# Seven block products in place of eight for the back products of the last layer's slice pairs

## The chip, the cores and the metric

The kernel runs on one core of a Trainium2 chip. The time is device microseconds (us) of one execution. A profile is one more execution, recorded by the hardware profiler; its span runs from the first to the last recorded instruction. PE is the matmul engine (TensorE), DVE is VectorE, ACT is ScalarE, POOL is GpSimd, SP issues DMAs.

## The reference, cut to what matters

```python
y = irfft(rfft(x, axis=1) * F)              # x is (2, 3008, 256), so 6016 tokens of 256
h = sigmoid(y @ w_gate) * (y @ w_val)       # 256 -> 1536
x2 = h @ w_out                              # 1536 -> 256
u = x2 @ w_in2                              # 256 -> 2048   (the last layer)
g = u * sigmoid(1.702 * u)
out = g @ w_out2                            # 2048 -> 256   (its back products)
```

Only the last layer, and in it the product `g @ w_out2`, is changed.

## The kernel before, in words

All matmuls are fp32-exact by splitting: each operand is a high part (rounded to the fp32r type) and a low part (what is left), and `mm3` makes three matmuls of a product: high by high, high by low, low by high. A tile has tokens along its columns: `tiles2` is ten tiles of 512 tokens and two of 448. Channels lie on the 128 partitions.

The last layer is the loop over `p` (six tile pairs, two tiles of tokens each) and, inside, over `fp` (eight slice pairs: 256 of the 2048 inner channels, two slices of 128). One pass, called a **set** here, makes a 2 by 2 product of blocks (two tiles, two halves of the 256 inputs, two slices). It is made with seven block products in place of eight, a scheme of Strassen's kind: sums of the inputs ("forms") were made ahead by DVE, sums of the weights too. The products go through `prod(o, k, first)`, in this order: `x` 0, `y` 4, `x` 5, `z` 1, `x` 6, `y` 2, `x` 3, where `x`, `y`, `z`, `w` are PSUM banks, and between them DVE and ACT do the sums that the scheme wants:

- after `x` 0: ACT copies the bank `x` to `s1`; product 5 is then accumulated onto the same bank;
- after `y` 4: ACT copies `y` to `s5`;
- after `x` 5: DVE makes `y = x + s5` (line 1772); after `z` 1: `z = z + s1` (line 1774); after `x` 6: `w = x + s5` (line 1782).

The four results `z`, `w`, `y`, `x` are the blocks (slice 0, tile 0), (1, 1), (0, 1), (1, 0). `Block.act` applies the activation twice by ACT: into the high part (line 1692) and in full precision into a tile `sg` (line 1693, two buffers); `Block.low` subtracts them by POOL (line 1696, both operands in SBUF). Then `Block.back(c)` multiplies a block by the output weights of its slice, half `c`, and accumulates in one of four PSUM banks `accs[tile][c]` (banks 4 to 7): eight back products a set, which are queued (`held`, `queue`) and issued by `back()` between the products of the next set. So a set has 15 groups of three matmuls on PE.

The order on every engine is that of the code: nothing is moved by a scheduler. "Chores" are pieces of other work that `spend(chores, n)` places at three points of a set, so many as `rate` says: in the last layer's later pairs, the forms of the next tile pair (DVE subtractions of SBUF tiles, ACT copies).

Of the kernel before, what the change touches and what calls it, by code (L numbers as in the profile page):

```python
# [17 lines left out]
P = 128  # L18
# [9 lines left out]
FC1 = DFF1 // P  # L28
# [61 lines left out]
def kernel(  # L90
# [1446 lines left out]
    def next_decode(j):  # L1537
        return decode_chores(j, st, lambda: [w[:, j % NWL] for w in wl] + [sp])

    def spend(q, n):  # L1540
        for k in range(n):
            if not q and bulk and not hold_back:
                q.extend(next_decode(bulk.pop(0)))
            if k and q and getattr(q[0], "apart", False):
                return
            chore(q)
# [5 lines left out]
    for p in range(FIRST, nt // 2):  # L1552
        n = tiles[2 * p][3]
        rhs = [[h[:, :n] for h in d] for d in sets[p]]
        for f in range(FC1):
# [8 lines left out]
            def prod(o, k, first):  # L1564
                mm3(o, lhs[k], rhs[k], first, True, skip_group_check=True)
# [114 lines left out]
    assert gn[0] % 4 == 0  # L1680
    gn[0] = 0

    class Block:
        def __init__(self, i, j, p, fp, bank):
            self.i, self.j, self.t, self.fp, self.bank = i, j, 2 * p + j, fp, bank
            self.n = tiles2[self.t]
            self.own = p == 0 and i == 0 and (fp > 0 or j == 0)

        def act(self):
            self.gp = [x[:, :self.n] for x in gslot()]  # L1690
            self.sg = self.bank if self.own else work.tile([P, 512], F32, tag="sg", name="sg")[:, :self.n]
# [3 lines left out]
        def low(self):  # L1695
            (nc.vector if self.own else nc.gpsimd).tensor_sub(self.gp[1], self.sg, self.gp[0].bitcast(F32))  # L1696

        def back(self, c):
            t, n, f = self.t, self.n, 2 * self.fp + self.i
            end = self.fp == FC2 // 2 - 1 and self.i != self.j  # L1700
            acc = accs[self.j][c][:, :n]
            mm3(acc, wp(f, c), self.gp, self.fp == 0 and self.i == self.j, end)
# [16 lines left out]
    LAST_S = 4  # L1719
    for p in range(nt // 2):  # L1720
        n = tiles2[2 * p]
        rhs = [[h[:, :n] for h in d] for d in (setB if p % 2 == 0 else setA)]
        asked = p + 1 == nt // 2
        for fp in range(FC2 // 2):
            x, z, w = (ps[ROT[(nset + k) % 3]][:, :n] for k in range(3))
            y = ps[2][:, :n]
            bz, by, bw, bx = (Block(i, j, p, fp, o) for (i, j), o in zip(((0, 0), (0, 1), (1, 1), (1, 0)), (z, y, w, x)))
            nset += 1
            if fp == 0:
                hold_back = False  # L1730
                while p and chores:
                    chore(chores)
            if p == 0:
                for g in (0, 1, 4, 5, 6, 2, 3):
                    if (fp or g not in (2, 3)) and 2 * g in done and g not in summed:
                        reload_s(g)
                for q in range(FC1):
                    if q in done and q not in placed:
                        reload(q)
                assert {2 * fp, 2 * fp + 1} <= placed and fp in summed  # L1740
                while 2 * fp + 1 not in done:
                    spend(chores, 1)
            lhs = w_parts(fp)
# [22 lines left out]
            queue += held  # L1766
            prod(y, 4, True)
            nc.scalar.copy(s5[:, :n], y)
            spend(chores, rate[0])
            back()  # L1770
            prod(x, 5, False)
# [5 lines left out]
            back()  # L1777
            spend(chores, rate[1])
# [7 lines left out]
            bw.low()  # L1786
            prod(y, 2, False)
# [10 lines left out]
            blocks = (bz, bw, by, bx) if fp or p == 0 else (bw, bz, by, bx)  # L1798
            held = [lambda o=o, c=c: o.back(c) for o in blocks for c in range(2)]
    queue += held  # L1800
    while queue:
        back()
# [41 lines left out]
```

## Time and profile before

| | before |
|---|---|
| time, median of 3 runs | 1134.05 us (1134.01 to 1134.63) |
| the profiled execution | 1133.56 us |
| its span | 1131.8 us |
| PE busy, matmul instructions | 1124.5 us (99%), 5072 |
| DVE, ACT, POOL busy | 694.0 us (61%), 641.6 us (57%), 408.9 us (36%) |
| mean granted clock of PE | 0.999 |

The profiled execution is 0.49 us under the median; 1.76 us of it lie outside the span. Busy time of an engine is an average over stages: DVE is busier in the first part of the program than in the last layer.

### The profile page before, as it was taken

The numbers are of one execution on the slowest core, as the hardware profiler recorded it, in microseconds if no ns is written. First come the engines' busy times: TensorE is split into PE (matmuls) and PEld (weight loads), VectorE is DVE, ScalarE is ACT, GpSimd is POOL, SyncE is SP. The second block draws the span as 40 slices with busy tenths as digits, with TensorE's granted clock in tenths as the row PEclk, the third lists the DMA queues.
The fourth block names the chain that finished last, engine by engine and source line by source line (L and its number), as shares of the span: only waits on it lengthen the run. The fifth ranks groups of instructions, "written<-read, shape, count | busy, mean of one in ns | idle before, by whom it ended". The sixth has DMA issues, their size and how long they took to land.

```text
span 1131.8 us, 14614 instructions
## 1 busy us (share of the span) xinstructions
PE 1124.5 (99%) x5072; PEld 905.0 (80%) x5072; DVE 694.0 (61%) x1171; ACT 641.6 (57%) x1221; POOL 408.9 (36%) x351
## 2 busy tenths in 40 slices
PE   9999999999999999999999999999999999999998
PEld 4378887677888888888888878888888888888897
DVE  6989998786688756787788788533224233233211
ACT  4655555554455644555655666756556556555554
POOL 3810004654333311211211132344555445544444
PEclk9999999999999999999999999999999999999999
DMA  9755238893200300126056250010100200200100
GB/s 208 200 182 180 93 122 226 195 182 80 80 1 1 109 1 1 41 94 118 31 191 210 95 178 31 28 47 1 57 19 1 75 1 1 70 1 1 38 1 33
DMA packets 84009, 91.21 MB, mean 81 GB/s; under 512 B 39072, under 2 KB 55968, under 8 KB 83936
## 3 DMA queue, kind: packets, MB, share of 16 engines
q1 hardware_dynamic: 81968, 87.37, 27.5%
q10 hardware_dynamic: 1968, 2.91, 0.8%
q8 instruction: 40, 0.66, 0.2%
q14 instruction: 33, 0.27, 0.1%
HBM read 55.52 MB, written 30.80 MB: 76 GB/s over the span
## 4 chain that ended last, share of the span: by engine, by line
PE 92%; DVE 2%; issue 1%; ACT 0%; DMA 0%; POOL 0%; ACTq 0%; DVEq 0%; POOLq 0%
PE ps L124 31%; PE ps L125 30%; PE ps L126 30%; PE ps L324 1%; DMA yraw<-tt 0%; DVE z L500 0%; DVE a L534 0%; DVE yp L1132 0%; POOL g L1696 0%; DVE ap L540 0%; DVE yraw L512 0%; DVE yraw L743 0%; DVE ps L560 0%; POOL v L550 0%; DVE v L479 0%
## 5 line engine op out<-in xcount | busy, mean ns | idle before, releaser
L1696 POOL TENSOR_TENSOR g<-sg,g 128x512 fp32r<-128x512 f32 (+1 forms) x117 | 150.0, 1295 | 178.4 <-ACT sg L1693 162.6
L1772 DVE TENSOR_TENSOR ps<-ps,tabs 128x512 f32<-128x512 f32 (+1 forms) x48 | 33.0, 688 | 213.4 <-PE ps L126 213.4
L121 POOL TENSOR_TENSOR g<-sg,g 128x512 fp32r<-128x512 f32 (+1 forms) x47 | 59.5, 1266 | 257.2 <-ACT g L120 257.2
L124 PE MATMUL ps<-yp,wg 128*128 128x512 f32 (+2 forms) x382 | 149.8, 393 | 0.0
L125 PE MATMUL ps<-yp,wg 128*128 128x512 f32 (+2 forms) x382 | 147.8, 387 | 0.0
L126 PE MATMUL ps<-yp,wg 128*128 128x512 f32 (+2 forms) x382 | 147.8, 387 | 0.0
L1692 ACT ACTIVATE g<-ps 128x512 fp32r<-128x512 f32 (+1 forms) x128 | 76.2, 595 | 84.6 <-DVE ps L1774 58.4
L125 PE MATMUL ps<-g,wo 128*128 128x512 f32 (+1 forms) x288 | 110.9, 386 | 0.0
L124 PE MATMUL ps<-g,wo 128*128 128x512 f32 (+1 forms) x288 | 110.9, 386 | 0.0
L126 PE MATMUL ps<-g,wo 128*128 128x512 f32 (+1 forms) x288 | 110.7, 386 | 0.0
L1696 POOL TENSOR_TENSOR wo<-sg,wo 128x512 fp32r<-128x512 f32 (+1 forms) x60 | 77.1, 1294 | 82.8 <-ACT sg L1693 82.6
L1693 ACT ACTIVATE sg<-ps 128x512 f32<-128x512 f32 (+1 forms) x177 | 105.5, 596 | 1.2 <-POOL g L1696 0.9
L124 PEld LDWEIGHTS ps<-yp,wg 128*128 128x128 f32 x382 | 71.7, 188 | 26.2 <-issue 13.0
L126 PEld LDWEIGHTS ps<-yp,wg 128*128 128x128 f32 x382 | 71.7, 188 | 14.3
L125 PEld LDWEIGHTS ps<-yp,wg 128*128 128x128 f32 x382 | 71.7, 188 | 13.0 <-issue 0.2
L124 PE MATMUL ps<-g,wg 128*128 128x512 f32 (+1 forms) x192 | 73.9, 385 | 0.0
L125 PE MATMUL ps<-g,wg 128*128 128x512 f32 (+1 forms) x192 | 73.9, 385 | 0.0
L126 PE MATMUL ps<-g,wg 128*128 128x512 f32 (+1 forms) x192 | 73.9, 385 | 0.0
L1629 ACT ACTIVATE sg<-ps 128x480 f32<-128x480 f32 (+1 forms) x48 | 28.1, 586 | 70.9 <-DVE ps L1627 70.9
L1692 ACT ACTIVATE wo<-ps 128x512 fp32r<-128x512 f32 (+1 forms) x64 | 38.2, 596 | 44.4 <-DVE ps L1774 30.3
L124 PEld LDWEIGHTS ps<-g,wo 128*128 128x128 f32 x288 | 54.0, 188 | 11.1 <-issue 0.8
L126 PEld LDWEIGHTS ps<-g,wo 128*128 128x128 f32 x288 | 54.0, 188 | 10.5
(304 smaller groups left out, 2778.4 us busy)
## 6 DMA issues: line engine op xcount, KB each, us to landing
yscr<-tt SPq DMA_DIRECT2D x56, 128.0 KB, 2.2
raw<-in_w_out_dram SPq DMA_DIRECT2D x14, 512.0 KB, 4.0
yraw<-xscr SPq DMA_DIRECT2D x14, 512.0 KB, 4.5
x<-in_xd_dram SPq DMA_DIRECT2D x32, 192.0 KB, 4.0
wscr<-wl SPq DMA_DIRECT2D x24, 256.0 KB, 2.0
wg<-wscr SPq DMA_DIRECT2D x24, 256.0 KB, 2.9
out_dram<-yraw SPq DMA_DIRECT2D x20, 256.0 KB, 2.2
f<-in_fd_dram SPq DMA_DIRECT2D x23, 192.0 KB, 4.6
```

Of the source, the lines that this page charges most:

```text
L121: lo_eng.tensor_sub(dst_lo, src, dst_hi.bitcast(F32))
L124: nc.tensor.matmul(out=o, lhsT=w[0], rhs=x[0], start=first, stop=False, **kw)
L125: nc.tensor.matmul(out=o, lhsT=w[0], rhs=x[1], start=False, stop=False, **kw)
L126: nc.tensor.matmul(out=o, lhsT=w[1], rhs=x[0], start=False, stop=last, **kw)
L324: nc.tensor.matmul(out=o[c], lhsT=w[64 * r:64 * r + n], rhs=x(r, k), start=True, stop=True, tile_position=(64 * r, 64 * k),)
L1629: nc.scalar.activation(out=sgz, in_=z, func=AF.Sigmoid)
L1692: nc.scalar.activation(out=self.gp[0], in_=self.bank, func=AF.Gelu_apprx_sigmoid)
L1693: nc.scalar.activation(out=self.sg, in_=self.bank, func=AF.Gelu_apprx_sigmoid)
L1696: (nc.vector if self.own else nc.gpsimd).tensor_sub(self.gp[1], self.sg, self.gp[0].bitcast(F32))
L1772: nc.vector.tensor_add(y, x, s5[:, :n])
```

## The change: what it does

The back product of a set is itself a 2 by 2 product of blocks (two tiles, two slices, two halves of the outputs). In some sets it is now made with seven block products too. These sets are `fp` 1, 2, 4 and 5 in the tile pairs `p` 2 to 5, and `fp` 4 and 5 in `p` 1: 18 sets, always two neighbours. I call the two the **first** and the **second** set, and the set behind them (`fp` 3 or 6) the **third**; `fp` 0 and 7 are plain, as is all of `p` 0.

- **Class Seven.** `after_y` and `after_x` make sums of the activated blocks instead of using them as they are: `t1 = y - z`, `t2 = w - t1`, `t3 = w - y`, `t4 = x - t2`, by DVE; their high parts by ACT copies (line 1733); the low parts of `t1`, `t2`, `t3` by POOL, those of `x` and `t4` by DVE. `third` and `fourth` do the high parts of `t3` and `t4` in the set after.
- **The products** `backs`: m3, m1, m6, m2, m7, m4, m5. Four of them (m1, m6, m7, and m5) go to the PSUM bank 3, `chain`; after each, `keep` reads that bank by DVE and adds it to one of four SBUF sums (`sums`; line 1868, or 1866 the first time). At `fp` 7 `fold` adds the sums to the accumulators by six DVE additions (line 1901).
- **Banks.** Bank 3 is taken by the chain. So for all sets of `p` 1 to 5 `x` and `z` alternate over two banks, and `w` is an `sg` tile in SBUF.
- **Weight sums.** `out_sums` makes the sums of the output weights of four slice pairs as chores in `p` 1 and at the beginning of `p` 2 (lines 1782 to 1799), and writes them to DRAM; `load_sout` loads three of them (six DMAs of 64 KB on SP's queue) for each of the 18 sets.
- **Rates** of the chores in `p` 1 to 5 are changed.

```diff
+    SEVEN = (1, 2, 4, 5)
+    OUT = {(1, 1): 4, (1, 2): 5, (1, 3): 1, (2, 0): 2}
...
+        def after_y(self):
+            z, y = self.z, self.y
+            y.full()
+            nc.vector.tensor_sub(z.sg, y.sg, z.sg)
+            self.t1.sg = z.sg
+            self.t1.high()
+            self.t1.low()
+
+        def after_x(self):
+            z, w, x, y = self.z, self.w, self.x, self.y
+            nc.vector.tensor_sub(self.e[0], w.sg, y.sg)
+            self.t3.sg = self.e[0]
+            nc.vector.tensor_sub(w.sg, w.sg, z.sg)
+            self.t2.sg = w.sg
+            x.take()
+            nc.scalar.activation(out=x.gp[0], in_=x.bank, func=AF.Gelu_apprx_sigmoid)
+            x.full()
+            x.low(nc.vector)
+            self.t2.high()
+            self.t2.low()
+            nc.vector.tensor_sub(self.e[1], x.sg, self.t2.sg)
+            self.t4.sg = self.e[1]
...
+            def keep(k):
+                dst = self.sums[k]
+                if not self.begun:
+                    nc.vector.tensor_copy(dst, self.chain)
+                else:
+                    nc.vector.tensor_add(dst, dst, self.chain)
...
+            return [m3, m1, m6, m2, m7, m4, m5]
...
-            rate = (2, 1, 1) if p else (3, 2, 2) if fp else (0, 0, 0)
+            if p:
+                if (p, fp) in OUT:
+                    out_jobs.append(OUT[p, fp])
+                if seven:
+                    rate = (0, 0, 0) if was else (3, 3, 0)
+                elif was:
+                    rate = 0, 1, 3
+                else:
+                    rate = (2, 2, 0) if fp == 0 else (0, 3, 3) if fp == LAST else (3, 3, 2) if fp == 3 else (2, 2, 2)
...
             nc.scalar.copy(s1[:, :n], x)
+            if was:
+                was.third()
...
             nc.scalar.copy(s5[:, :n], y)
+            if was:
+                was.fourth()
             spend(chores, rate[0])
...
+            if was:
+                was.fourth_low()
...
             spend(chores, rate[1])
             if not bz.own:
                 bz.low()
             prod(x, 6, False)
-            nc.vector.tensor_add(w, x, s5[:, :n])
+            if p:
+                bw.bank = bw.hold()
+            nc.vector.tensor_add(bw.bank, x, s5[:, :n])
...
-            by.act()
-            spend(chores, rate[2])
-            by.low()
+            if seven:
+                if was:
+                    load_sout(fp, 1)
+                seven.after_y()
+            else:
+                by.act()
+                spend(chores, rate[2])
+                by.low()
             prod(x, 3, False)
-            bx.act()
-            bx.low()
-            back()
+            if seven:
+                back()
+                seven.after_x()
+            else:
+                bx.act()
+                bx.low()
+                back()
             back()
```

What stands where on DVE, between the middle of a second set and the beginning of a third (`p` 3, `fp` 5 and 6). Before, one set in the same tile pair (line 1132 is a chore):

```order
L1772 TENSOR_TENSOR ps_73<-ps_71,tabs 128x512 [waits PE_49,Activation_49]
L1774 TENSOR_TENSOR ps_72<-ps_72,s_2834 128x512 [waits PE_49]
L1132 TENSOR_TENSOR sx_2826<-yraw,sx_2825 128x512
L1782 TENSOR_TENSOR ps_74<-ps_71,tabs 128x512 [waits PE_49]
L1132 TENSOR_TENSOR sx_2826<-yraw,sx_2825 128x512 [waits DVE_49,Activation_49]
```

Now (the second set's `w` sum is line 2008, line 1737 with `spare` is t4's low part, line 1134 a chore; `ps_74` is the chain):

```order
L2008 TENSOR_TENSOR sg<-ps_72,tabs 128x512 [waits PE_49,Pool_49]
L1868 TENSOR_TENSOR sums<-sums,ps_74 128x512 [waits PE_49]
L1825 TENSOR_TENSOR sg<-ps_73,sg 128x512 [waits Activation_49,Pool_49]
L1868 TENSOR_TENSOR sums<-sums,ps_74 128x512 [waits PE_49]
L1832 TENSOR_TENSOR spare<-sg,ps_73 128x512
L1834 TENSOR_TENSOR sg<-sg 128x512 [waits DVE_49,Pool_49]
L1737 TENSOR_TENSOR g_2873<-ps_72,g_2872 128x512 [waits Activation_49]
L1842 TENSOR_TENSOR spare<-ps_72,sg 128x512 [waits DVE_49]
L1868 TENSOR_TENSOR sums<-sums,ps_74 128x512 [waits PE_49]
L1992 TENSOR_TENSOR ps_73<-ps_71,tabs 128x512 [waits PE_49,Activation_49]
L1994 TENSOR_TENSOR ps_72<-ps_72,s_2835 128x512 [waits PE_49]
L1868 TENSOR_TENSOR sums<-sums,ps_74 128x512 [waits PE_49]
```

Between two sets' own sums there was one chore or none; now a `keep` (line 1868) that waits for m5, the last group of the set, stands ahead of the subtractions for t3 (1832) and t2 (1834), and the latter has both inputs in SBUF.

ACT at the same place; before, two activations, each twice, and then the copy to `s1`:

```order
L1692 ACTIVATE wo_85<-ps_73 128x512 [waits PE_49]
L1693 ACTIVATE sg<-ps_73 128x512 [waits Pool_49]
L1127 ACTIVATE yp_2639<-xs 128x448
L1692 ACTIVATE wo_85<-ps_71 128x512 [waits PE_49]
L1693 ACTIVATE sg<-ps_71 128x512 [waits Pool_49]
L1760 COPY s_2834<-ps_72 128x512 [waits PE_49]
```

Now (line 1728 `y` and `x` in full, 1733 the high parts of t1, t2, t3, 1837 the high part of `x`):

```order
L1728 ACTIVATE ps_73<-ps_73 128x512 [waits PE_49]
L1733 ACTIVATE wo_86<-sg 128x512 [waits DVE_49]
L1837 ACTIVATE ks_1645<-ps_72 128x512 [waits PE_49,Pool_49]
L1728 ACTIVATE ps_72<-ps_72 128x512
L1733 ACTIVATE g_2872<-sg 128x512 [waits DVE_49]
L1970 COPY s_2835<-ps_71 128x512 [waits PE_49]
L1733 ACTIVATE wo_86<-spare 128x512
```

The copy to `s1` (line 1970) now stands behind the high part of t2, which waits for DVE.

DVE in `p` 1, `fp` 1, where the weight sums are made; these rows are new, and a plain set had no work there before but its three sums:

```order
L1992 TENSOR_TENSOR ps_73<-ps_72,tabs 128x512 [waits PE_49,Activation_49]
L1994 TENSOR_TENSOR ps_71<-ps_71,s_2835 128x512 [waits PE_49]
L1792 TENSOR_TENSOR wr<-wv 128x128
L1793 TENSOR_TENSOR wr<-wv,wr 128x128 [waits DVE_49]
L1799 TENSOR_TENSOR wlo<-wr,wh 128x512 [waits Activation_49]
L2008 TENSOR_TENSOR sg<-ps_72,tabs 128x512 [waits PE_49,Pool_49]
```

The low part of the weight sums (line 1799, both inputs in SBUF) stands ahead of the sum into `w` (2008).

## Rows read from the trace of the kernel before

**Rows 1.** The page: busy time by engine; busy time of stretches of the last layer.

```profile
PE 1124.5 (99%) x5072; PEld 905.0 (80%) x5072; DVE 694.0 (61%) x1171; ACT 641.6 (57%) x1221; POOL 408.9 (36%) x351
745.00:827.00 82.00, 82.00 (x363) 67.91 (x362) 27.17 (x37) 47.38 (x89) 41.82 (x33) 1.00 0.08 26
909.00:991.00 82.00, 82.00 (x364) 67.89 (x363) 27.15 (x37) 47.77 (x90) 41.58 (x32) 1.00 0.08 25
```

**Rows 2.** Waits from 640 to 1132 us, those of PE's weight loads (all).

```profile
PEld ps L124 <- ACT s L1760: 0.5, 1, 0.5
PEld ps L124 <- ACT sg L1693: 0.5, 1, 0.5
PEld ps L124 <- DVE ps L1772: 0.4, 1, 0.4
PEld ps L124 <- DVE g L1696: 0.2, 1, 0.2
```

**Rows 3.** Timeline, PE: start, duration, then what (512 columns; 448 columns).

```profile
848.15 0.39 PE L124 MATMUL ps<-sx,wo 128*128 128x512 f32 x1
848.37 0.39 PE L125 MATMUL ps<-sx,wo 128*128 128x512 f32 x1
848.60 0.39 PE L126 MATMUL ps<-sx,wo 128*128 128x512 f32 x1
848.83 0.39 PE L124 MATMUL ps<-sx,wg 128*128 128x512 f32 x1
...
1090.22 0.36 PE L124 MATMUL ps<-g,wg 128*128 128x448 f32 x1
1090.42 0.36 PE L125 MATMUL ps<-g,wg 128*128 128x448 f32 x1
```

**Rows 4.** Timeline of one set, DVE, ACT and POOL; in brackets idle time and releaser.

```profile
849.10 0.70 DVE L1772 TENSOR_TENSOR ps<-ps,tabs 128x512 f32<-128x512 f32 x1 [5.85 <-PE ps L126]
849.71 0.70 DVE L1774 TENSOR_TENSOR ps<-ps,s 128x512 f32<-128x512 f32 x1
850.31 0.68 DVE L1132 TENSOR_TENSOR yp<-yraw,yp 128x512 fp32r<-128x512 f32 x1
851.75 0.70 DVE L1782 TENSOR_TENSOR ps<-ps,tabs 128x512 f32<-128x512 f32 x1 [0.75 <-PE ps L126]
852.35 1.09 DVE L1132 TENSOR_TENSOR yp<-yraw,yp 128x512 fp32r<-128x512 f32 x1
850.44 0.60 ACT L1692 ACTIVATE wo<-ps 128x512 fp32r<-128x512 f32 x1 [1.14 <-DVE ps L1774]
850.93 0.59 ACT L1693 ACTIVATE sg<-ps 128x512 f32<-128x512 f32 x1
851.61 1.29 POOL L1696 TENSOR_TENSOR wo<-sg,wo 128x512 fp32r<-128x512 f32 x1 [4.37 <-ACT sg L1693]
```

**Rows 5.** Timeline around a wait of PE for the copy to s1.

```profile
653.31 0.58 ACT L1760 COPY s<-ps 128x512 f32<-128x512 f32 x1
653.43 0.40 PE L126 MATMUL ps<-g,wg 128*128 128x512 f32 x1
653.94 0.51 PE L124 MATMUL ps<-sx,wo 128*128 128x512 f32 x1
654.28 0.39 PE L125 MATMUL ps<-sx,wo 128*128 128x512 f32 x1
```

**Rows 6.** Timeline, DVE and POOL where both work at once.

```profile
793.89 1.65 DVE L1132 TENSOR_TENSOR sx<-xs,sx 128x512 fp32r<-128x512 f32 x1 [1.65 <-ACT sx L1127]
793.70 3.00 POOL L1696 TENSOR_TENSOR g<-sg,g 128x512 fp32r<-128x512 f32 x2
833.08 0.69 DVE L1142 TENSOR_TENSOR xs<-yraw,xs 128x512 f32<-128x512 f32 x1
833.25 1.67 POOL L1696 TENSOR_TENSOR g<-sg,g 128x512 fp32r<-128x512 f32 x1 [0.75 <-ACT sg L1693]
```

**Rows 7.** The page, DMA issues of 64 KB: issue, count, size, us to landing.

```profile
yraw<-tt SPq DMA_DIRECT2D x12, 64.0 KB, 3.7
```

More of the change, by code (lines that the diff above doesn't have):

```diff
@@ L1543, in spend @@
                 q.extend(next_decode(bulk.pop(0)))
+            elif not q and out_jobs:
+                q.extend(out_sums(out_jobs.pop(0)))
             if k and q and getattr(q[0], "apart", False):
@@ L1681, with gtake, give @@
     gn[0] = 0
+    frees = list(gring)
+    spares = []
+    def gtake():
+        return frees.pop(0)
+    def give(slot, p):
+        if p and slot is gring[0]:
+            assert not spares
+            spares.extend(work.tile([P, 512], F32, tag=f"g{i}", name="spare", bufs=4) for i in range(2))
+        else:
+            frees.append(slot)
     class Block:
@@ L1687, in __init__, with take, hold, full @@
             self.own = p == 0 and i == 0 and (fp > 0 or j == 0)
-        def act(self):
-            self.gp = [x[:, :self.n] for x in gslot()]
-            self.sg = self.bank if self.own else work.tile([P, 512], F32, tag="sg", name="sg")[:, :self.n]
+            self.sg = None
+        def take(self):
+            self.slot = gtake()
+            self.gp = [x[:, :self.n] for x in self.slot]
+        def hold(self):
+            self.sg = work.tile([P, 512], F32, tag="sg", name="sg")[:, :self.n]
+            return self.sg
+        def act(self):
+            self.take()
+            if self.own:
+                self.sg = self.bank
+            elif self.sg is None:
+                self.hold()
             nc.scalar.activation(out=self.gp[0], in_=self.bank, func=AF.Gelu_apprx_sigmoid)
             nc.scalar.activation(out=self.sg, in_=self.bank, func=AF.Gelu_apprx_sigmoid)
-        def low(self):
-            (nc.vector if self.own else nc.gpsimd).tensor_sub(self.gp[1], self.sg, self.gp[0].bitcast(F32))
+        def full(self):
+            nc.scalar.activation(out=self.bank, in_=self.bank, func=AF.Gelu_apprx_sigmoid)
+            self.sg = self.bank
+        def high(self):
+            self.take()
+            nc.scalar.activation(out=self.gp[0], in_=self.sg, func=AF.Copy)
+        def low(self, eng=None):
+            eng = eng or (nc.vector if self.own else nc.gpsimd)
+            eng.tensor_sub(self.gp[1], self.sg, self.gp[0].bitcast(F32))
         def back(self, c):
@@ L1701, in back @@
             acc = accs[self.j][c][:, :n]
-            mm3(acc, wp(f, c), self.gp, self.fp == 0 and self.i == self.j, end)
+            mm3(acc, wp(f, c), self.gp, self.fp == 0 and self.i == self.j, end, skip_group_check=True)
+            if c:
+                give(self.slot, now[0])
             if end:
@@ L1717, in back, with load_sout, out_sums, whole @@
                 )
-    LAST_S = 4
+    sout = [
+        [wo[i][:, FC1 - 1, :P] for i in range(2)],
+        [wo[i][:, FC1 - 1, P:] for i in range(2)],
+        [sx0[i][:, 5, :] for i in range(2)],
+    ]
+    def load_sout(fp, *ks):
+        q = SEVEN.index(fp)
+        for k in ks:
+            for i in range(2):
+                nc.sync.dma_start(out=sout[k][i].bitcast(F32), in_=oscr[q, i, :, k * P:(k + 1) * P])
+    def out_sums(fp):
+        w = slot(2 * fp + 1)
+        q = SEVEN.index(fp)
+        one, two = ("ex", "c") if q % 2 == 0 else ("c", "ex")
+        t = {}
+        def whole():
+            t["v"] = st.tile([P, 512], F32, tag=one, name="wv")
+            nc.vector.tensor_add(t["v"], *[x.bitcast(F32) for x in w])
+        def sums():
+            v = t["v"].rearrange("p (c i m) -> p c i m", c=2, m=P)
+            r = t["r"] = st.tile([P, 4, P], F32, tag=two, name="wr")
+            nc.vector.tensor_add(r[:, 0], v[:, 0, 1], v[:, 1, 1])
+            nc.vector.tensor_sub(r[:, 1], r[:, 0], v[:, 0, 0])
+        def more():
+            v, r = t["v"].rearrange("p (c i m) -> p c i m", c=2, m=P), t["r"]
+            nc.vector.tensor_sub(r[:, 2], v[:, 0, 0], v[:, 0, 1])
+            nc.vector.tensor_sub(r[:, 3], v[:, 1, 0], r[:, 1])
+            t["hi"] = st.tile([P, 512], F32R, tag="m", name="wh")
+            nc.scalar.activation(out=t["hi"], in_=r.rearrange("p k m -> p (k m)"), func=AF.Copy)
+        def low():
+            lo = st.tile([P, 512], F32R, tag=one, name="wlo")
+            nc.vector.tensor_sub(lo, t["r"].rearrange("p k m -> p (k m)"), t["hi"].bitcast(F32))
+            for i, x in enumerate((t["hi"], lo)):
+                nc.sync.dma_start(out=oscr[q, i], in_=x[:, P:].bitcast(F32))
+                nc.sync.dma_start(out=w[i][:, P:2 * P].bitcast(F32), in_=x[:, :P].bitcast(F32))
+        def rest():
+            pass
+        steps = [lambda fn=fn: fn() for fn in (whole, sums, more, low, rest)]
+        for step in steps:
+            step.out = True
+        return steps
@@ new lines, with __init__, third, fourth @@
+    class Seven:
+        def __init__(self, p, fp, n, bz, by, bw, bx):
+            self.begun = fp != SEVEN[2 * (p == 1)]
+            self.fp, self.n = fp, n
+            self.z, self.y, self.w, self.x = bz, by, bw, bx
+            self.t1, self.t2, self.t3, self.t4 = (Block(0, 0, p, fp, None) for _ in range(4))
+            self.chain = ps[3][:, :n]
+            self.e = [b[:, :n] for b in spares]
+            self.sums = [b[:, :n] for b in sums_out]
+        def after_y(self):
[19 more added lines that the diff above has]
+            self.t4.sg = self.e[1]
+        def third(self):
+            self.t3.high()
+            self.t3.low()
+        def fourth(self):
+            self.t4.high()
+        def fourth_low(self):
+            self.t4.low(nc.vector)
+        def backs(self):
+            n, fp = self.n, self.fp
+            c11, c21, c12, c22 = (accs[j][c][:, :n] for j in range(2) for c in range(2))
+            def mm(o, w, b, first=False):
+                mm3(o, w, b.gp, first, True, skip_group_check=True)
+                give(b.slot, now[0])
+            def keep(k):
[4 more added lines that the diff above has]
+                    nc.vector.tensor_add(dst, dst, self.chain)
+            def m3():
+                mm(c12, sout[2], self.w)
+            def m1():
+                mm(self.chain, wp(2 * fp, 0), self.z, True)
+                keep(0)
+            def m6():
+                mm(self.chain, sout[0], self.t2)
+                keep(1)
+            def m2():
+                mm(c11, wp(2 * fp + 1, 0), self.x)
+            def m7():
+                mm(self.chain, sout[1], self.t3)
+                keep(2)
+            def m4():
+                mm(c21, wp(2 * fp + 1, 1), self.t4)
+            def m5():
+                mm(self.chain, wp(2 * fp, 1), self.t1, True)
+                keep(3)
+            return [m3, m1, m6, m2, m7, m4, m5]
+        def fold(self, k):
+            c11, c21, c12, c22 = (accs[j][c][:, :self.n] for j in range(2) for c in range(2))
+            m1, u2, u3, m5 = self.sums
+            for o, a in (((c12, u2), (c22, u3)), ((c12, m5), (c22, m5)), ((c11, m1), (c21, u3)))[k]:
+                nc.vector.tensor_add(o, o, a)
@@ L1720 @@
+    LAST = FC2 // 2 - 1
+    seven = None
+    now = [0]
     for p in range(nt // 2):
+        now[0] = p
         n = tiles2[2 * p]
@@ L1723 @@
         asked = p + 1 == nt // 2
+        if p == 1:
+            assert not raws and not bulk
+            sums_out = [st2.tile([P, 2, 512], F32, tag="raw", name="sums", bufs=2) for _ in range(2)]
+            sums_out = [b[:, k] for b in sums_out for k in range(2)]
+            frees.append(ks)
         for fp in range(FC2 // 2):
-            x, z, w = (ps[ROT[(nset + k) % 3]][:, :n] for k in range(3))
             y = ps[2][:, :n]
+            if p == 0:
+                x, z, w = (ps[ROT[(nset + k) % 3]][:, :n] for k in range(3))
+            else:
+                x, z = (ps[(nset + k) % 2][:, :n] for k in range(2))
+                w = None
             bz, by, bw, bx = (Block(i, j, p, fp, o) for (i, j), o in zip(((0, 0), (0, 1), (1, 1), (1, 0)), (z, y, w, x)))
             nset += 1
+            was, seven = seven, Seven(p, fp, n, bz, by, bw, bx) if p and fp in SEVEN[2 * (p == 1):] else None
             if fp == 0:
                 hold_back = False
-                while p and chores:
+                while p and chores and not hasattr(chores[0], "out"):
                     chore(chores)
@@ L1742 @@
                     spend(chores, 1)
+            if seven and not was:
+                load_sout(fp, 2, 0, 1)
             lhs = w_parts(fp)
@@ L1766 @@
             queue += held
+            if seven and was:
+                load_sout(fp, 2)
+            if fold:
+                fold(0)
             prod(y, 4, True)
             nc.scalar.copy(s5[:, :n], y)
+            if was:
+                was.fourth()
             spend(chores, rate[0])
             back()
+            if fold:
+                fold(1)
             prod(x, 5, False)
@@ L1777 @@
             back()
+            if was:
+                was.fourth_low()
+            if seven and was:
+                load_sout(fp, 0)
             spend(chores, rate[1])
@@ L1786 @@
             bw.low()
+            if fold:
+                fold(2)
             prod(y, 2, False)
```

15 lines of the change are left out of this document (13 added, 2 removed).

## The prediction

> **What bounds the kernel now.** I read the page first, for the engine that is always busy: PE, 99% of the span [rows 1]. Then the busy times of stretches of the last layer: PE is busy for the whole of every stretch, at a granted clock of 1.00, while DVE works a third of the time, ACT 58% and POOL half [rows 1]. Then the waits: in the whole last layer PE's weight loads waited four times, 1.6 us in all [rows 2], so there is next to nothing to win by better hiding; the layer ends sooner only with fewer matmuls. Last the timeline, for the pace: matmuls of 512 columns start every 0.227 us, so a group of three takes 0.68 us; with 448 columns 0.203 and 0.61 [rows 3]. A set of 15 groups is 10.2 us.
>
> A set works because its sums are early enough. The timeline of one set gives the steps of which all below is made [rows 4]. DVE starts on a group 0.43 to 0.50 us after the start of its last matmul (848.60 in [rows 3] to 849.10), so about 0.90 after the group's start. DVE instructions with a PSUM operand follow one another at 0.61. ACT starts 0.73 after the start of the DVE sum that it needs (849.71 to 850.44), its instructions follow at 0.49 and last 0.59, POOL starts 0.68 after ACT's start (850.93 to 851.61) and takes 1.29.
>
> **What is removed.** One group in each of 18 sets: 14 of 512 columns and 4 of 448. 14 x 3 x 0.227 + 4 x 3 x 0.203 = 11.97 us. As nothing hides PE now, all of it is gained unless PE comes to wait.
>
> **What is added, and where it hides.** A first or second set has 14 or 15 groups on PE and more of everything else: up to 13 DVE instructions, some 8 to 9 us, 13 on ACT, 7 us, 5 on POOL, 6.5 us, in a second set of 9.5 us. In total it fits. What counts is the order, so I walked through it with the steps above.
>
> The second set, from its start. Groups: x6 at 5.44, y2 6.12, m7 6.80, m4 7.48, x3 8.16, m5 8.84; the third set starts at 9.52. The `w` sum starts at 5.44 + 0.90 = 6.34, the two activations of `w` at 7.07 and 7.56, that of `y` at 8.05, over at 8.65. DVE makes t1 at 8.69, ACT its high part at 9.42, POOL its low part from 10.10 to 11.39. DVE's next instruction is the `keep` of m5, which can't start before 8.84 + 0.90 = 9.74. Behind it stand the subtraction for t3 (10.35) and that for t2 (10.96). On ACT the copy to `s1` of the third set stands behind the high part of t2, and x5 of the third set, at 9.52 + 2.72 = 12.24 if nothing waits, must wait for that copy.
>
> The subtraction for t2 has both inputs in SBUF and meets POOL. Such a DVE instruction takes 0.68 alone and 1.09 when POOL is at work (850.31 and 852.35 [rows 4]): POOL was at it until 852.90, the instruction ended at 853.44, so 0.54 after POOL. The same with a longer wait: 1.65 us behind a POOL instruction that had started 0.19 earlier [rows 6]. And the other way round POOL waits: started 0.17 after DVE, it took 1.67 in place of 1.29 [rows 6]. DVE's sums with one PSUM operand kept 0.70 beside POOL (851.75 [rows 4]). So t2 ends at 11.39 + 0.55 = 11.94. The high part starts at 11.97, the copy at 12.46, ends at 13.05. PE goes on 0.05 after the end of such a copy, and its second matmul then comes 0.34 later, not 0.23 [rows 5]. So x5 starts at 13.10, and the loss is 0.86 + 0.11 = 0.97. The second activation of `w` is now in place on an SBUF tile and waits for ACT itself; a full 0.60 in place of 0.49 puts POOL's end, and with it the loss, at 1.1. I take **1.05**. If POOL were not in the way, t2 would end at 11.64 and the loss be 0.67: that is the lower bound. There are nine such places (one in `p` 1, two in `p` 2 to 5): 9 x 1.05 = **9.5 us**, bounds 6.0 and 10. (The bank `y` is also late, read by the subtraction for t3 until 11.05, y4 due at 10.88; that is inside the same wait.)
>
> The Trainium skill (SBUF — State Buffer, Who interferes with whom) has the rule for this: a DVE instruction with two SBUF inputs and a GpSimd instruction that reads SBUF take a shared port in turn, and the one that comes second is blocked for the whole of the other. By that rule t2 would start afresh at POOL's end and take its full 0.68; the rows show 0.54, so the trace has part of it overlapped. By the rule the nine places would cost 1.2 us more; the sum goes by the rows.
>
> From the first to the second set there is no `keep` in between: t1 at 8.69, t3 at 9.30, t2 at 9.91, and POOL asks for the port at 10.10, 0.19 later. ACT does x at 9.91 and 10.40, the high part of t2 at 10.89, the copy 11.38 to 11.97, and x5 is due at 12.92. No loss; 0.3 each, 2.6 us in all, if POOL came first there.
>
> **Weight sums.** In three sets (`p` 1, `fp` 1 and 2; `p` 2, `fp` 0) their low part stands ahead of the `w` sum. POOL has the low part of `z` from 6.18 to 7.47 (z sum at 4.28, activations 5.01 and 5.50, then 0.68). ACT's high part of the weight sums ends at 6.6, so DVE meets POOL and ends at 8.02. The `w` sum then reads the bank `x` until 8.67, and x3 onto that bank, due at 8.16, starts at 8.72: 0.56 + 0.11 = 0.67 each, **2.0 us**. Bounds: nothing and 2.0.
>
> **A chore in the third sets.** In seven third sets (`fp` 6 of `p` 1, `fp` 3 and 6 of `p` 2 to 4) one chore on SBUF tiles stands ahead of the `w` sum, behind a `keep` and t4's low part. Counted from the z sum: keep 0.68, t4 1.29, the chore 1.90; and POOL's low part of `z` also at 0.73 + 0.49 + 0.68 = 1.90. It is a tie. If POOL is first, the chore ends at 1.90 + 1.29 + 0.55 = 3.74, the `w` sum at 4.4, and x3, due 3.88 after the z sum, loses 0.6 + 0.1: 7 x 0.7 = 4.9 us. In four of the seven nothing but DVE's own order holds the chore, while POOL has to be told by ACT; I take DVE first, **nothing**, and keep both ends.
>
> **At no cost.** The DMA loads of weight sums: one 64 KB load lands in 3.7 us [rows 7], and each is issued a set (9.5 us) before its use, when the set's m3, m6 or m7 has freed the place; if that cover went, PE would wait a few us at each. The additions of `fold` (six, 0.61 each) stand at `fp` 7, four of them before DVE's sum of x5: they end at about 3.4, that sum is due at 3.62. In plain sets `w` in SBUF and two banks for `x` and `z`: the bank of `x` is free when ACT has read it, about 1 us into the next set, and the product that needs it comes at 3.4.
>
> **Sum.** 1133.56 - 11.97 + 9.5 + 2.0 = 1133.1 for the profiled execution; the runs' median is 0.49 above it, so **1133.6 us**. A difference of 0.2%, 2.3 us, is about what a measurement of this kernel can tell from no change: I forecast no change.
>
> **Rivals.**
> - POOL wins the tie in the third sets: 1133.6 + 4.9 = 1138.5, slower. For it: the rows put both at the same instant, and a chore that waits for a DMA or for ACT comes later still. Against it: 0.05 us decides. It decides from the moment when POOL has started as the chore comes. Chance 0.28.
> - The port is not what holds t2, because POOL is earlier or later than I have it, and the weight sums' low part or the copy finds slack: 9 x 0.67 = 6.0, with 2.0 or without: 1130.1 or 1128.1. For it: the walk moves by tenths with every step, and each tenth at nine places is 0.9 us. Chance 0.27.
> - The work hides altogether, so that the whole of 11.97 is gained: 1122.1; or most of it, 1122 to 1127. For it speaks only that the engines' sums fit. Against it: the `keep` of m5 can't be earlier than its matmul. Chance 0.08.
>
> No change for lack of effect is left out: the matmuls are gone from PE's row.
>
> **How the numbers follow.** The forecast has 0.37; its own range is 1131.3 to 1136. Faster than 0.2% is the second and third rival, 0.35; slower the first, 0.28. The range that leaves out no more than 2 in 10 goes from 1127 (the third rival out) to 1139 (both late at once, and the first sets too, out).
>
> **What would show it.** PE: 54 matmuls fewer. The waits of PE's weight loads: some 9 waits for the copy to `s1` (now line 1970) of 0.8 to 1.1 us, at the third sets, and DVE's t2 (line 1834) at 0.9 to 1.1 us there and 0.68 in the first sets. Three waits for the `w` sum (line 2008) of 0.5 us in `p` 1 and 2, and up to seven more in the third sets if POOL is first. I am wrong if the waits for the copy are missing or under 0.5 us, if waits for the loads of weight sums appear, or if PE waits for the chain (a `keep`) inside a set.

## The result, and the profile after

The changed kernel takes 1140.62 us (median of four runs, 1139.58 to 1142.29), the kernel before 1134.22 in runs beside it (four, 1134.01 to 1134.63): a ratio of 1.0057 with a 95% interval of 1.0040 to 1.0075. It is slower by 0.57%, 1.6 us beyond the end of my range. The profiled execution took 1139.59 us with a span of 1137.5, at a granted clock of 1.00. One execution told of below (of the kernel "odd sets, sums apart") took 1865.81 us at a mean granted clock of 0.556; nothing here explains it, and it is in no ratio.

The page of the changed kernel, busy time by engine, answers to the first row of [rows 1]:

```profile
PE 1120.8 (99%) x5018; PEld 893.4 (79%) x5018; DVE 845.8 (74%) x1405; ACT 674.0 (59%) x1279; POOL 443.0 (39%) x369
```

The 54 matmuls are gone. The 12 us that they took are more than given back in waits. Here are all waits of PE's weight loads from 640 us on (line waited for: us, times, longest), where there were four of 1.6 us [rows 2]:

```profile
PEld ps L126 <- ACT s L1970: 12.8, 15, 1.2
PEld ps L126 <- DVE spare L1832: 3.9, 9, 0.4
PEld ps L126 <- DVE sg L2008: 3.6, 4, 1.2
PEld ps L126 <- DVE ps L1901: 1.1, 1, 1.1
PEld ps L126 <- ACT sg L1725: 0.5, 1, 0.5
PEld ps L126 <- DVE ps L1992: 0.4, 1, 0.4
PEld ps L126 <- DVE g L1737: 0.2, 1, 0.2
```

And two stretches of the last layer (busy time of PE, weight loads, DVE, ACT, POOL; granted clock; DMA), which answer to the last two of [rows 1]: PE now stands still for 1.6 us in the second, and for 2.9 in the first, which holds weight sums and a fold as well.

```profile
745.00:827.00 82.00, 79.07 (x342) 63.40 (x342) 56.37 (x79) 50.40 (x95) 45.09 (x33) 1.00 0.15 48
...
909.00:991.00 82.00, 80.40 (x349) 64.69 (x348) 56.91 (x83) 54.10 (x101) 49.25 (x36) 1.00 0.15 48
```

A wait ends when a semaphore is up, and PE then needs a little more, so I took the loss from the starts of the matmuls in PE's timeline: each distance between two starts less the pace of 0.227 or 0.203 [rows 3], where it is over 0.06. I call the sum of these the lost starts. From 740 us on the kernel before loses nothing, the changed one 16.6 us: 11.7 at the nine places where a third set follows a second (1.27 to 1.32 each, of which 0.3 fall on y4 and 1.0 on x5), 1.95 at three weight sums (0.62, 0.62, 0.71), 1.92 at `fp` 7 of `p` 1, and 0.9 elsewhere: 0.33 and 0.34 at two of the places where a second set follows a first, 0.11 at `fp` 7 of `p` 2 and of `p` 3. Another 0.9 are a few ns each, most of them in the ten matmuls behind each wait. 16.6 + 0.9 - 11.97 is +5.5. To compare runs I use the **last layer**, the span less the start of its first sum of x5 (646.9 us before, 647.0 after): 484.9 us before, 490.5 after, +5.6.

One of the nine places, second to third set in `p` 2; the third set starts at 838.70. The timelines of DVE, ACT, POOL and PE of the changed kernel (start, duration, engine, line; idle time and releaser in brackets):

```profile
838.18 0.69 DVE L1825 TENSOR_TENSOR sg<-ps,sg 128x512 f32<-128x512 f32 x1 [0.63 <-ACT ps L1728]
838.90 0.69 DVE L1866 COPY sums<-ps 128x512 f32<-128x512 f32 x1
839.50 0.68 DVE L1832 TENSOR_TENSOR spare<-sg,ps 128x512 f32<-128x512 f32 x1
840.28 1.16 DVE L1834 TENSOR_TENSOR sg<-sg 128x512 f32<-128x512 f32 x1
...
836.29 0.63 ACT L1724 ACTIVATE ks<-sg 128x512 fp32r<-128x512 f32 x1 [1.01 <-DVE sg L2008]
836.96 0.63 ACT L1725 ACTIVATE sg<-sg 128x512 f32<-128x512 f32 x1
837.49 0.58 ACT L1728 ACTIVATE ps<-ps 128x512 f32<-128x512 f32 x1
838.90 0.63 ACT L1733 ACTIVATE g<-sg 128x512 fp32r<-128x512 f32 x1 [0.83 <-DVE sg L1825]
...
841.48 0.63 ACT L1733 ACTIVATE g<-sg 128x512 fp32r<-128x512 f32 x1 [0.97 <-DVE sg L1834]
842.02 0.57 ACT L1970 COPY s<-ps 128x512 f32<-128x512 f32 x1
...
839.61 1.28 POOL L1737 TENSOR_TENSOR g<-sg,g 128x512 fp32r<-128x512 f32 x1 [0.66 <-PE ps L128]
...
841.50 0.40 PE L128 MATMUL ps<-g,wg 128*128 128x512 f32 x1
842.64 0.49 PE L126 MATMUL ps<-sx,wo 128*128 128x512 f32 x1 [0.74 <-ACT s L1970]
842.97 0.39 PE L127 MATMUL ps<-sx,wo 128*128 128x512 f32 x1
```

Read it from the end. The last of these matmuls but one is x5, 1.14 after its predecessor; it starts 0.05 after the copy's end (842.59). The copy stood behind t2's high part (841.48), that behind t2 (841.44), and t2 took 1.16 because POOL made t1's low part until 840.89: it ends 0.55 after POOL. DVE reached t2 so late because the `keep` at 838.90 and t3 stood ahead. That is the chain that the prediction walked. What it had too short is the front: t1 comes at 838.18, 0.52 before the third set; forecast was 0.83 before it. That lateness passes on through POOL and not through the `keep`: the `keep` starts at 838.90, where the walk had it (9.74 into a set that began at 829.18 is 838.92), while POOL starts 0.33 later than walked. So the `keep` hardly waits for m5 any more, 0.11 at most; what it costs t3 and t2 is above all its own turn on DVE, 0.61.

The place that the prediction left out, `fp` 7 of `p` 1, on DVE:

```profile
796.58 1.65 DVE L1134 TENSOR_TENSOR sx<-xs,sx 128x512 fp32r<-128x512 f32 x1 [1.34 <-ACT sx L1129]
798.16 0.67 DVE L1868 TENSOR_TENSOR sums<-sums,ps 128x512 f32<-128x512 f32 x1
798.76 2.48 DVE L1901 TENSOR_TENSOR ps<-ps,sums 128x512 f32<-128x512 f32 x4
...
803.79 1.38 DVE L1793 TENSOR_TENSOR wr<-wv,wr 128x128 f32<-128x128 f32 x1
805.10 0.68 DVE L2008 TENSOR_TENSOR sg<-ps,tabs 128x512 f32<-128x512 f32 x1
...
803.63 1.40 POOL L1737 TENSOR_TENSOR ks<-sg,ks 128x512 fp32r<-128x512 f32 x1 [4.23 <-ACT sg L1725]
```

The additions of `fold` come behind a chore that waited for ACT and then for POOL, and PE, which would have gone on at 799.88, went on at 800.69. The `w` sum comes behind five steps of the weight sums, one of them a 128x128 subtraction (line 1793) that took 1.38 beside POOL in place of 0.28; PE lost another 1.0 there.

### The profile page after: what moved, and what is told of

It is laid out like the page before. It is cut to its first block, busy times and chain, and to the rows that moved or that the text cites. A ratio compares the mean times of both kernels' runs of the same rounds, so it can differ in the third digit from the quotient of the medians.

```text
span 1137.5 us, 15244 instructions
## 1 busy us (share of the span) xinstructions
PE 1120.8 (99%) x5018; PEld 893.4 (79%) x5018; DVE 845.8 (74%) x1405; ACT 674.0 (59%) x1279; POOL 443.0 (39%) x369
## 4 chain that ended last, share of the span: by engine, by line
PE 83%; DVE 7%; ACT 3%; issue 1%; DMA 1%; POOL 0%; DVEq 0%; SPq 0%; ACTq 0%; POOLq 0%
PE ps L126 28%; PE ps L127 27%; PE ps L128 27%; PE ps L326 1%; DVE sg L1834 1%; ACT sg L1725 1%; DVE sums L1868 1%; ACT s L1970 0%; DVE spare L1832 0%; ACT g L1733 0%; DVE sg L2008 0%; DMA yraw<-tt 0%; DVE ps L1992 0%; DVE ps L1994 0%; DVE yraw L1148 0%
## 5 line engine op out<-in xcount | busy, mean ns | idle before, releaser
L1737 POOL TENSOR_TENSOR g<-sg,g 128x512 fp32r<-128x512 f32 (+1 forms) x92 | 123.7, 1349 | 133.9 <-ACT sg L1725 106.6
L123 POOL TENSOR_TENSOR g<-sg,g 128x512 fp32r<-128x512 f32 (+1 forms) x47 | 59.5, 1267 | 257.1 <-ACT g L122 257.1
L127 PE MATMUL ps<-g,wo 128*128 128x512 f32 (+1 forms) x305 | 117.4, 386 | 0.0
L126 PE MATMUL ps<-g,wo 128*128 128x512 f32 (+1 forms) x305 | 117.4, 386 | 0.0
L128 PE MATMUL ps<-g,wo 128*128 128x512 f32 (+1 forms) x305 | 117.3, 386 | 0.0
L1669 DVE TENSOR_TENSOR g<-ps,g 128x480 fp32r<-128x480 f32 (+1 forms) x48 | 32.4, 675 | 48.7 <-ACT g L1666 48.6
L126 PEld LDWEIGHTS ps<-g,wo 128*128 128x128 f32 x305 | 57.2, 188 | 11.8 <-issue 0.8
L128 PEld LDWEIGHTS ps<-g,wo 128*128 128x128 f32 x305 | 57.2, 188 | 11.0
L127 PEld LDWEIGHTS ps<-g,wo 128*128 128x128 f32 x305 | 57.2, 188 | 10.9
L1724 ACT ACTIVATE g<-ps 128x512 fp32r<-128x512 f32 (+1 forms) x63 | 37.1, 589 | 40.2 <-DVE ps L1994 38.4
L1725 ACT ACTIVATE sg<-ps 128x512 f32<-128x512 f32 (+1 forms) x101 | 59.5, 589 | 0.7 <-POOL g L1737 0.2
L126 PE MATMUL ps<-yp,sx 128*128 128x512 f32 (+2 forms) x129 | 50.4, 390 | 2.4 <-ACT s L1970 2.2
L1737 POOL TENSOR_TENSOR ks<-sg,ks 128x512 fp32r<-128x512 f32 (+1 forms) x28 | 37.9, 1355 | 32.3 <-ACT sg L1725 26.2
```

The source lines that it names most:

```text
L123: lo_eng.tensor_sub(dst_lo, src, dst_hi.bitcast(F32))
L1669: nc.vector.tensor_sub(g0[1], x, g0[0].bitcast(F32))
L1737: eng.tensor_sub(self.gp[1], self.sg, self.gp[0].bitcast(F32))
```

## The experiments

My theory: the loss sits where a third set follows a second, and its root is the `keep` of m5, which stands ahead of t3 and t2 on DVE and lets POOL take the port first. Rivals: the order on ACT (the copy behind t2's high part) is enough to explain it; or the port alone is; or the seven-block sets cost as much wherever they stand. The first four kernels ran beside one another.

**Copy first.** t2's high and low parts are made behind the copy to `s1`; the products that use them come later.

```diff
             x.low(nc.vector)
-            self.t2.high()
-            self.t2.low()
...
         def third(self):
+            self.t2.high()
+            self.t2.low()
             self.t3.high()
...
-            return [m3, m1, m6, m2, m7, m4, m5]
+            return [m3, m1, m2, m6, m7, m4, m5]
```

> High and low part of t2 are made in the next set, behind the copy to s1, and m2 goes ahead of m6. If the chain keep of m5, t2, its high part, copy to s1 is what PE waits for: the nine waits of x5 (1.0 us each with the late second matmul) go, the nine of y4 (0.3) stay: 1140.6 - 9 = 1131.6 us. If the added work as a whole (DVE, ACT and POOL too full, the loads of weight sums) is what costs, the order of one instruction changes little: 1139 to 1142, with waits elsewhere.

1157.81 us, ratio 1.0201 (1.0186 to 1.0216): missed on both sides. The wait for the copy did shrink, from 12.8 to 4.0 us, but others grew, 33.2 us of lost starts in all. The largest, and a place on DVE and POOL that shows how the first of them comes about:

```profile
PEld ps L126 <- DVE sg L2008: 11.5, 17, 1.2
PEld ps L126 <- DVE spare L1832: 7.0, 9, 0.8
PEld ps L126 <- DVE spare L1840: 6.2, 11, 0.7
PEld ps L126 <- ACT s L1970: 4.0, 5, 1.0
```

```profile
1011.71 1.77 DVE L1737 TENSOR_TENSOR g<-spare,g 128x512 fp32r<-128x512 f32 x1
1013.40 0.68 DVE L2008 TENSOR_TENSOR sg<-ps,tabs 128x512 f32<-128x512 f32 x1
...
1011.64 1.29 POOL L1737 TENSOR_TENSOR wo<-sg,wo 128x512 fp32r<-128x512 f32 x1 [1.30 <-ACT sg L1725]
```

DVE's low part of t4 now comes 0.07 after POOL took up a low part, takes 1.77, and the `w` sum waits behind it. At this place PE loses 0.47 to that low part itself and 0.15 to the `w` sum; where a chore also stands between the two, the `w` sum costs some 0.7. So moving the copy doesn't mend the place, it moves the wait. I did not trace the other waits one by one.

**Keep later.** The `keep` of m5 stands behind t2's difference; nothing else moves.

```diff
                 mm(self.chain, wp(2 * fp, 1), self.t1, True)
-                keep(3)
+                late.append(lambda: keep(3))
...
             nc.vector.tensor_sub(w.sg, w.sg, z.sg)
+            while late:
+                late.pop()()
```

> The keep of m5 stands behind the subtractions for t3 and t2 on DVE. If that keep's wait for m5 is the root: t3 and t2 are 0.9 us earlier, both waits (x5 and y4, 1.3 us at each of nine places, 11.7 us) go: 1129 us, less a small new wait of m1 for the keep (0.1 to 0.2 each): 1129 to 1131. If the port is the root and not the keep, t2 meets POOL all the same and half of the waits stay: 1134 or more. If the added work as a whole: 1139 to 1142.

1131.32 us, ratio 0.9969 (0.9957 to 0.9981), 0.3 over the upper end of what was expected; last layer 481.6, 8.9 less than with the change as it was. The same place in this kernel, DVE and POOL:

```profile
837.90 0.69 DVE L1825 TENSOR_TENSOR sg<-ps,sg 128x512 f32<-128x512 f32 x1 [0.63 <-ACT ps L1728]
838.51 0.68 DVE L1832 TENSOR_TENSOR spare<-sg,ps 128x512 f32<-128x512 f32 x1
839.29 0.69 DVE L1834 TENSOR_TENSOR sg<-sg 128x512 f32<-128x512 f32 x1
839.90 0.69 DVE L1868 COPY sums<-ps 128x512 f32<-128x512 f32 x1
...
839.34 3.06 POOL L1737 TENSOR_TENSOR g<-sg,g 128x512 fp32r<-128x512 f32 x2 [0.66 <-PE ps L128]
```

t2 starts 1.39 after t1, 0.71 earlier than with the change as it was: 0.61 for the turn of the `keep` and 0.1 for its wait. It starts 0.05 before POOL and takes 0.69; now POOL waits (two low parts in 3.06, where one takes 1.29). Of 1.30 per place 0.30 are left on average (0.27 to 0.37), and for another reason: m1 opens the chain's bank anew and waits for the late `keep`. So the place of the `keep` in DVE's order is the root, less its wait for m5 than its own turn and the meeting with POOL that follows from it.

**Low part later.** The rival that the port does it, with the `keep` where the change put it: POOL makes t1's low part behind t2's.

```diff
             self.t1.high()
-            self.t1.low()
...
             self.t2.low()
+            self.t1.low()
```

> POOL makes the low part of t1 behind that of t2, so that it is not at work when DVE makes t2. The port's share alone: t2 takes 0.68 in place of 1.16 us, x5 comes 0.5 earlier at nine places: 1140.6 - 4.3 = 1136.3 us. If the port were the whole cause, the waits for the copy would go: 1131.6. If it has no part, 1140.6; if POOL's later low parts now hold m7 or m5, waits for POOL show and the time is 1140 or more.

1144.48 us, ratio 1.0085 (1.0068 to 1.0102). At the nine places it did what was expected: t2 takes 0.69, and x5's part of the loss falls from 0.91 to 0.44, so the port is half of that part and the `keep`'s own time the other half. But POOL's work came later, and the tie in the third sets, which DVE had won, was lost; PE's waits for the `w` sum, and in the same `p` 2 DVE and then POOL:

```profile
PEld ps L126 <- DVE sg L2008: 10.0, 11, 1.2
...
846.13 0.90 DVE L1737 TENSOR_TENSOR ks<-spare,ks 128x512 fp32r<-128x512 f32 x1
846.95 1.78 DVE L1140 TENSOR_TENSOR xs<-yraw 128x512 f32<-128x512 f32 x1
848.65 0.68 DVE L2008 TENSOR_TENSOR sg<-ps,tabs 128x512 f32<-128x512 f32 x1
...
845.17 1.30 POOL L1737 TENSOR_TENSOR wo<-spare,wo 128x512 fp32r<-128x512 f32 x1
846.73 1.45 POOL L1737 TENSOR_TENSOR g<-sg,g 128x512 fp32r<-128x512 f32 x1 [0.25 <-ACT sg L1725]
```

The chore takes 1.78, the `w` sum comes late, and PE's waits for it go from 3.6 us (4) to 10.0 (11): one more in each of the seven third sets with a chore. Lost starts are 21.0 us, 4.4 more than with the change as it was: the nine places give back 4.2, the seven third sets add 5.3, and 3.3 come in the sets behind them and elsewhere. This is the mechanism that the prediction had as its rival on the slower side: real, but not in the change as it was made.

**Single sets.** Only slice pairs 1 and 4 (4 alone in `p` 1) are done by seven products: nine sets, none next to another, and two weight sums in place of four.

```diff
-    SEVEN = (1, 2, 4, 5)
+    SEVEN = (1, 4)
...
-    OUT = {(1, 1): 4, (1, 2): 5, (1, 3): 1, (2, 0): 2}
+    OUT = {(1, 1): 4, (1, 3): 1}
```

> Seven products only at fp 1 and 4 (9 sets, no two neighbours; the weight sums of two slice pairs in place of four). There is no second set, so no keep between t1 and t2. If the waits belong to the second sets: 9 groups saved (6.0 us), no waits for the copy, 1 to 2 us for the weight sums in p 1: 1129 to 1131 us. If each set with seven products costs its 0.65 us wherever it stands (full engines, loads): half of the loss, 1134.2 - 6.0 + 8.7 = 1137.

1130.79 us, ratio 0.9967 (0.9954 to 0.9980), as expected. Half of the saving (5.98 us) less 2.2 of lost starts gives 3.8, and the last layer is 3.8 shorter than before (481.1). The rival that a set costs the same wherever it stands is out: without a neighbour it costs nothing but its weight sums.

**Keep later, sums apart.** The second experiment, and the third and fourth steps of the weight sums are each kept from being run right behind another chore, so that DVE doesn't meet POOL ahead of the `w` sum; at `fp` 0 two chores may come after y's product.

```diff
+        steps[2].apart = steps[3].apart = True
...
-                    rate = (2, 2, 0) if fp == 0 else (0, 3, 3) if fp == LAST else ...
+                    rate = (2, 2, 2) if fp == 0 else (0, 3, 3) if fp == LAST else ...
```

> The keep of m5 behind t2, as in the run before, and besides the steps of the weight sums kept apart, so that their low part no longer stands ahead of the sum into w. If the three waits of 0.6 to 0.7 us (and one of 1.0 at fp 7 of p 1) come from that order: 1131.3 - 2.9 = 1128.4 us. If they come from the sums' mere presence on DVE: 1131.3.

1129.13 us, ratio 0.9952 (0.9936 to 0.9968), last layer 478.6. The last layer is 3.0 shorter than in the second experiment, as expected; of the 0.7 over the expected time 0.6 lie ahead of that layer (its first sum of x5 is at 648.3, there at 647.7). PE waits for the `w` sum nowhere any more; lost starts 4.6 us.

**Odd sets**, 1, 3 and 5 (3 and 5 in `p` 1), 14 in all with no neighbours and three weight sums, and **odd sets, sums apart**, with the edits on the weight sums' steps and on the rate at `fp` 0 of the kernel just told (the `keep` of m5 stays where the change put it).

```diff
-    SEVEN = (1, 2, 4, 5)
+    SEVEN = (1, 3, 5)
...
-    OUT = {(1, 1): 4, (1, 2): 5, (1, 3): 1, (2, 0): 2}
+    OUT = {(1, 1): 3, (1, 2): 5, (1, 3): 1}
```

> Seven products at fp 1, 3 and 5 (fp 3 and 5 in p 1), 14 sets and again no two neighbours. If only neighbours cost: 9.3 us saved, 2 to 4 us of waits for the weight sums and for chores in the first sets: 1127 to 1129 us. If it is the density of such sets (3 of 8 in place of 2, DVE and POOL fuller): waits for the copy or for the sum into w in many sets, 1131 or more.

> fp 1, 3 and 5 with the weight sums' steps apart. Both effects add: 1125 to 1127 us; by density 1129 or more.

1131.92 us, ratio 0.9982 (0.9973 to 0.9992), and 1130.33, ratio 0.9964 (0.9953 to 0.9974): both some 3 us above the upper end of what I expected, and in the range that I had given to the rival by density. The waits speak against that rival: those for the copy are 2.7 and 2.3 us in all (0.5 at most each), and lost starts are 5.8 and 4.5 us, more than half of them at `fp` 7 of `p` 1. The profiled execution of the first took 1133.77, and its last layer begins 2.4 us later than before (first sum of x5 at 649.3, before at 646.9). In both kernels PE waited over 2 us for the `fold` of `p` 1, where three steps of the weight sums, each slowed by POOL to 1.26 to 1.82, stood ahead of the last `keep`. And in the second the clock fell behind that wait; windows of PE, weight loads, DVE, ACT and POOL, granted clock and DMA, and then PE's matmuls:

```profile
799.00:802.00 3.00, 1.05 (x5) 0.88 (x6) 3.00 (x6) 0.00 (x0) 0.00 (x0) 1.00 0.00 0
802.00:805.40 3.40, 3.40 (x10) 2.62 (x9) 2.08 (x6) 1.89 (x4) 1.27 (x1) 0.50 0.06 23
805.40:809.00 3.60, 3.60 (x17) 2.99 (x16) 1.48 (x3) 3.04 (x6) 2.45 (x2) 1.00 0.38 124
```

```profile
798.57 0.39 PE L128 MATMUL ps<-yp,wl 128*128 128x512 f32 x1
800.95 0.50 PE L126 MATMUL ps<-g,wl 128*128 128x512 f32 x1 [1.99 <-DVE ps L1902]
...
802.38 0.63 PE L128 MATMUL ps<-g,wl 128*128 128x512 f32 x1
802.80 0.63 PE L126 MATMUL ps<-yp,sp 128*128 128x512 f32 x1
```

From 802.0 to 805.4 the granted clock is 0.50, the lower of its two levels (1.2 of 2.4 GHz), and matmuls start 0.43 apart in place of 0.227: 1.55 us more.

**Odd sets, lighter** and **keep, lighter**: the wait of the `fold` taken away, by one chore in place of three after y's product at `fp` 6 of `p` 1, in the odd kernel with sums apart and in the one with the later `keep` and sums apart.

```diff
-                    rate = 0, 1, 3
+                    rate = (0, 1, 1) if (p, fp) == (1, 6) else (0, 1, 3)
```

> As the kernel with single sets 1, 3 and 5, but at slice pair 6 of the second tile pair one chore after y's product in place of three: the weight sums' first two steps come behind the last keep and the first fold on DVE. If DVE's order is what the two folds' product waited for there (2.25 us), that wait goes, and if the granted clock of 0.50 behind it followed from the gap, that goes too (1.55 us): the last layer takes 480.5 - 3.8 = 476.7 us, and the waits of the weight loads name DVE ps of the fold line no longer, or with under 0.5 us. If the clock fell for another reason, a stretch at 0.50 stays and the layer takes about 478. If the wait only moves (the w sum of slice pair 7 stands behind the same steps, at 1.3 us or so), about 478 too, with the wait under the w sum's line.

> The same edit on the kernel with neighbours 1, 2 and 4, 5, the keep behind t2's difference and the weight sums' third and fourth steps apart. There the fold waited 0.92 us, behind a forming step of the next tile pair that took 1.65 beside POOL. Last layer 478.6 - 0.9 = 477.7 us, so about 1128.2 where the part before the last layer takes what it took; 1129.1 again if the wait only moves to the w sum of slice pair 7. No stretch of a granted clock under 1.00 in either case, since the gap there was already under 1 us.

1126.07 us, ratio 0.9925 (0.9911 to 0.9938), and 1126.88, ratio 0.9936 (0.9922 to 0.9950). Last layers 476.7 and 477.7, both as expected. These are all waits of the weight loads in the odd kernel:

```profile
PEld ps L126 <- ACT s L1971: 2.3, 7, 0.5
PEld ps L126 <- ACT sg L1725: 0.5, 1, 0.5
PEld ps L126 <- DVE ps L1993: 0.4, 1, 0.4
PEld ps L126 <- DVE g L1737: 0.2, 1, 0.2
```

The wait for the `fold` is gone and the clock stays at 1.00 throughout. The rival by density is out: 14 sets with seven products lose 0.8 us of starts in all. Both versions beat the kernel before; which of the two is faster their intervals, which overlap, don't tell. The odd sets save 11 x 0.68 + 3 x 0.61 = 9.3 us and lose 0.8 of it from 740 us on; the neighbours save 12.0 and lose 3.7 there, 2.6 of it in m1's wait for the late `keep`.

## Why the prediction was wrong

**Right.** The saving, 11.97 us; that PE would give most of it back at the nine places, through the copy to `s1`, and the chain of causes there; the three weight sums (1.95 lost, forecast 2.0); DVE first in the third sets, so that no wait stands there; no wait for a load of the weight sums; no cost of the two banks and of `w` in SBUF in the plain sets.

**The term that was mis-sized** is the nine places: 9 x 1.05 = 9.5, upper bound 10; measured 1.30 each, 11.7. The step that failed is the start of t1. I set the second activation of `w`, in place in SBUF, at 0.60 after the first at most; it came 0.67 after it (836.96). The steps to the `w` sum, `y` and t1 were each 0.04 to 0.05 later than walked. Together t1 was 0.31 later, POOL's end 0.32, the copy's end 0.36. From there the walk held: t2 ends 0.55 after POOL (0.55 forecast; it took 1.16 and not 0.98, as POOL was later than walked by 0.33 and t2 by 0.14), x5 0.05 after the copy, 0.10 for its second matmul. The bound was no bound, because it let one step be 0.11 slower (the second activation alone was 0.18 later than at a distance of 0.49) and not the whole chain of five.

The Trainium skill (SBUF — State Buffer, Who interferes with whom) has DVE with two SBUF inputs blocked while POOL holds the shared port. In this trace t2 ends 0.55 after POOL's end, less than the 0.68 that it takes alone; so it is not blocked for all of it, and the rows' 0.54 was the better figure for the sum.

**What was left out.** At `fp` 7 of `p` 1 I had the `fold` at no cost (its additions over at about 3.4, needed by 3.62), 0.2 to spare, and I counted only `fold`'s own additions, not the chore ahead of them; and I priced the weight sums only where their low part stands ahead of the `w` sum, not where the steps before it do. Those two cost 1.9. Where a second set follows a first I forecast nothing, or 0.3 each if POOL came first; 0.33 and 0.34 were lost at two such places, where ACT made chores of the next tile pair ahead of `w`'s activations (two of line 1129, 1.15 us from 856.39): the first activation of `w` comes 1.43 after its sum there (856.00 to 857.43), 0.72 at the place shown above. t2 took 0.69 there (860.76), so it was not POOL. At the first sets of `p` 1 and `p` 4 the same two chores cost nothing; in `p` 1 they were over early enough (`w` 0.73 after its sum). This is read from the trace, no run moved these chores.

The sum with the measured terms: -11.97 + 11.7 + 1.95 + 1.9 + 0.9 + 0.9 of slower pace behind waits is +5.4; the last layer measured +5.6. Forecast was -0.5. So of the 5.9 between the two sums 2.2 are the nine places, and 3.7 are terms that I had put at nothing, the `fold` of `p` 1 and the steps behind it foremost. The chance of slower (0.28) stood on the third sets' tie alone, and the time came out slower for another reason.

**Open.** Why the part before the last layer, which the change leaves alone, differs between kernels by up to 2.4 us (646.9 to 649.3) isn't settled. Nor is what the medians add to the last layer (6.4 between them, 5.6 in the layer), and neither is each of the waits of the first experiment.

## What to carry to other kernels

On an engine that executes in order, what stands ahead delays all that stands behind: put an instruction that only clears a buffer behind those that something waits for, and check by one move whether it is the root. When a walk over several steps gives a loss that repeats at many places, a few hundredths at most steps and two tenths at one make a quarter of the loss; the bound must let all steps be late together. And a saving that fills the gaps between stages can be worth more in part than whole: 14 sets with plain ones between them save 9.3 us and keep 8.2, 18 sets with neighbours save 12.0 and lost 5.6 net, and keep 7.2 with their order mended.

## What the runs showed of the hardware

- Two starts of PE 2.38 us apart were followed, 1.05 us on, by 3.4 us at a granted clock of 0.50 in the profiled execution of one kernel (odd sets, sums apart; mean granted clock 0.998, as in six of the seven others of it that took some 1130 us). In the odd kernel without the sums apart 2.40 us (801.08 to 803.48) left it at 1.00.
- Behind a wait the second matmul comes 0.10 to 0.11 late, at every one of the places, and the next ten a few ns each.
- A 128x128 subtraction on DVE, 0.28 us alone, takes 1.38 when POOL holds the port: the price of meeting POOL hangs mostly on what POOL still has to do. It ends 0.14 after POOL (805.17, 805.03), and the 128x512 t2 0.55 after: each some 0.14 less than it takes alone.
- An activation in place on a tile in SBUF came 0.67 after the one before it that reads the same tile, and the activation on a PSUM bank behind it 0.53 later; in [rows 4] the pair follows at 0.49.
